# Threshold attention and a gated feed-forward block: every stage as tasks of one engine, ordered by a list scheduler

## The chip, the core and the metric

The kernel runs on one core of a Trainium2 chip. A core has a matrix engine (PE, with its weight loads listed as PEld), a vector engine (DVE), an engine for activation functions (ACT), a general engine (POOL) and SP, which here only issues DMAs. Each engine works through its own queue in the order in which the program was written, and waits at an instruction until the semaphores that it needs have arrived. The metric is the time of one execution in microseconds (us).

## What is computed

```python
# q, k, v: (8, 8, 576, 64) f32; 64 heads, two heads are one "pair"
scores = q @ k.T / sqrt(64)
thresh = max(scores, -1) - tau                 # tau = 0.02
scores = where(scores >= thresh, scores, -1e9)
attn   = exp(scores - max); attn /= sum(attn, -1) + 1e-9
x      = (attn @ v) reshaped to (4608, 512)
h      = x @ w_in                              # (512, 2048), given as 64-bit floats
g      = h * sigmoid(1.702 * h)
out    = g @ w_out                             # (2048, 512), given as 64-bit floats
```

## The kernel before

**Attention.** There are 32 pairs n (four for each of the eight sequences). Of the 576 keys, 512 are four main tiles t of 128 and the last 64 of both heads share one tail tile. For a pair, DVE transposes q and k (`prep`, L206); PE makes the scores with keys on the partitions (`scores`, L233 and L222) into PSUM tiles `ps` of the pool psA, which has three buffers; ACT copies them to SBUF (L239, L226) as `s_m` (seven buffers) or `s_t`. DVE takes the maximum over groups of 32 keys of each tile (`in_groups`, L254), folds the parts into one threshold a query (`over_groups`, `thresholds`) and spreads it over the partitions as `mb` (L282). Then DVE subtracts `mb` from each tile (`sub`, L291 and L294), and ACT runs a very steep Prelu, which is the mask, and the exp (`exps`, L300 and L301). When all five tiles are done, PE multiplies by the values (`values`, `pv`, L315). The row sums come, for the first six pairs (`BY_PE`), from a second pass of PE over the five tiles with a matrix of ones (`sums_by_pe`, `den`, also L315), which DVE then reads (L337), and for the others from DVE (`in_groups` again, as a sum). `place_x` (L366) multiplies `pv` by the reciprocal sums into `xT`.

**Feed-forward.** The 4608 rows are nine blocks of 512. A block needs the pairs of its sequences. It has 16 products with w_in (`mm1`, tile `hps`, L379), each of four matmuls in two parts; behind each, ACT makes a tanh (`th`, L386) and DVE the gated product `gT` (L387). Then it has four products with w_out (`mm2`, tile `ops`, L395) of 16 matmuls in eight parts, which ACT halves (`osb`, L401) and SP stores. `hps` and `ops` share the pool psM, which has two buffers. A matmul in f32 shows as two records in the trace: 128 records of hps and 128 of ops for each block.

**Weights.** w_in and w_out arrive as 64-bit floats and are converted in 64 pieces (`convert`): two DMAs, two DVE steps (L162, L172), one of ACT (L167), two of POOL (L176, L179), one of DVE (L188) and one of POOL (L192), with the piece that was begun one call earlier finished first.

**What sets the order.** All engines are scheduled by hand: what the program writes first stands first in each queue. A list `plan` holds (place, function) entries and is sorted by place. A pair begins at `LEN * n` with `LEN = 18`, and its steps stand at fixed distances from there, for instance

```python
at(t0 + 1.5 * t, scores, n, t)
at(t0 + 9.0 + 1.3 * t, exps, n, t)
at(t0 + 18.6, values, n)
```

The parts of a block are spread evenly between the moment at which its pairs are ready and that of the next block. A function of the plan writes for several engines at once: `exps` is Prelu and exp in a row, the second part of `mm1` also writes the tanh and gT, and `scores` also writes the copies.

Of the kernel before, what the change touches and what calls it, by code (L numbers as in the profile page):

```python
# [17 lines left out]
P = 128  # L18
GELU_SCALE = 1.702
EPS = 1e-9  # L20
# [8 lines left out]
def kernel(  # L29
# [66 lines left out]

    raws, vs = {}, {}

    def load_pair(n, queues):
        b, hp = divmod(n, NPAIR)  # L100
        raws[n] = []
        for (name, src), queue in zip((("q", q), ("k", k)), queues):
            t = work.tile([P, QB, 32], FP32, name=f"{name}_raw", tag=f"{name}_raw", bufs=1)
            for h in range(2):
                for j in range(2):
                    queue.dma_start(
                        out=t[ds(64 * h + 32 * j, 32), :, :],
                        in_=src[b, 2 * hp + h, :, ts(j, 32)].rearrange(
                            "(c p) d -> p c d", p=32
                        ),  # L110
                    )
            raws[n].append(t)
# [18 lines left out]
    staged, opened = [], []  # L131
    n_loaded = [0]

    def load_w():
        if n_loaded[0] == len(pieces):
            return
        dst, src, c, j = pieces[n_loaded[0]]
        n_loaded[0] += 1
        part = dst[:, c, ts(j, WC)]
        dram = src[ts(c, P), ts(j, WC)]  # L140
        if not wide:
            nc.sync.dma_start(out=part, in_=dram)
            return
# [9 lines left out]
        staged.append((t, t3, part))  # L153

    def convert_w():

        if not staged:
            return
        t, t3, part = staged.pop(0)
        hi = t[:, :, 1]  # L160
# [3 lines left out]
        )  # L164

        mant = work.tile([P, WC], FP32, name="mant", tag="mant")
        nc.scalar.activation(  # L167
            out=mant, in_=frac, func=AF.Copy, bias=1.0, scale=2.0**-28
        )

        ex = work.tile([P, WC], U32, name="ex", tag="ex")
        nc.vector.tensor_scalar(  # L172
            out=ex, in0=hi, scalar1=20, scalar2=0x7FF,
            op0=ALU.logical_shift_right, op1=ALU.bitwise_and,
        )
# [6 lines left out]
        opened.append((t, part, mant, ex))  # L182

    def convert_w_end():
        if not opened:
            return
        t, part, mant, ex = opened.pop(0)
# [4 lines left out]
        nc.gpsimd.tensor_tensor(out=part, in0=mant, in1=ex.bitcast(FP32), op=ALU.mult)  # L192

    def convert():
        convert_w_end()
        convert_w()
        load_w()


    mats, sT, stats, mbs = {}, {}, {}, {}  # L200

    def prep(n, which):

        src = raws[n][which]
        dst = work.tile([P, S], FP32, name="qkT", tag=f"qkT{which}", bufs=1)
        nc.vector.transpose(out=dst, in_=src.rearrange("p c d -> p (c d)"))  # L206
        mats.setdefault(n, []).append(dst)
        if which == 1:
            for h in range(2):
                nc.scalar.copy(out=kd[n % 2][ts(h, D), ts(h, D)], in_=dst[ts(h, D), MAIN:S])  # L210
            del raws[n]
# [4 lines left out]
    def scores(n, t):  # L216
        qT, kT = mats[n]
        if t == NKT:
            st = work.tile([P, S], FP32, name="s_t", tag="s_t", bufs=2)
            ps = psA.tile([P, 2, 512], FP32, name="ps", tag="ps")  # L220
            for c in range(2):
                nc.tensor.matmul(  # L222
                    ps[:, c, 0:SH], lhsT=kd[n % 2], rhs=qT[:, ts(c, SH)],
                    start=True, stop=True,
                )
            nc.scalar.copy(out=halves(st), in_=ps[:, :, 0:SH])  # L226
            del mats[n]
        else:
            st = work.tile([P, 2, S], FP32, name="s_m", tag="s_m", bufs=7)
# [8 lines left out]
            for h in range(2):  # L238
# [201 lines left out]

    LEN = 18.0
    BY_PE = 6
    plan = []
# [82 lines left out]
```

## Time and profile before

| | us |
|---|---|
| median of 3 runs (1716.7 to 1718.14) | 1717.1 |
| the profiled execution | 1718.59 |
| its span | 1716.8 |
| PE busy in the span | 1477.6 (86%) |
| DVE busy | 979.5 (57%) |
| ACT busy | 673.0 (39%) |
| POOL busy | 117.1 (7%) |

A busy time is the sum of an engine's instructions; for PE it contains the time in which matmuls run at a lower granted clock. The granted clock of a stretch is the share of TensorE's full speed. A wait is put down to the instruction whose semaphore came last.

### The profile page before, as it was taken

The page shows a single profiled execution, that of the slowest core. Times are in us where ns is not written, and L with a number is a line of the kernel's source. Part 1 is how long each engine was busy: PE and PEld are TensorE (multiplying, and loading weights), DVE is VectorE, ACT ScalarE, POOL GpSimd, SP SyncE. Part 2 cuts the span into 40 slices and gives each one's busy share as a digit, 9 for nine tenths or more (in the row PEclk, how much of TensorE's full clock was granted, in tenths as well). Part 3 has the DMA queues.
Part 4 walks back from the last instruction along what each step waited for, and adds up shares of the span by engine and source line. Part 5 has one row for each costly group of instructions (what it writes and reads, how often), then busy time and mean ns, then how long its engine had stood idle before and what let it go on. Part 6 is the DMA issues. An engine that isn't in the chain of part 4 may idle for free.

```text
span 1716.8 us, 14214 instructions
## 1 busy us (share of the span) xinstructions
PE 1477.6 (86%) x4976; PEld 677.1 (39%) x4976; DVE 979.5 (57%) x1698; ACT 673.0 (39%) x917; POOL 117.1 (7%) x204
## 2 busy tenths in 40 slices
PE   4647475799889978997899799998899789999998
PEld 2323132344334433443344344444344334444443
DVE  4664646486666666666577566766577567510110
ACT  4453424244344444444444433543444444310110
POOL 0014645400000000000000000000000000000000
PEclk8877787899989998999899999999899989999999
DMA  3215555411111111111111100210111110000000
GB/s 55 58 45 135 163 172 160 156 34 33 21 21 33 34 21 21 28 39 21 21 28 33 28 6 16 45 25 18 21 33 34 21 21 20 13 0 13 13 6 19
DMA packets 214295, 72.22 MB, mean 42 GB/s; under 512 B 193232, under 2 KB 201424, under 8 KB 214224
## 3 DMA queue, kind: packets, MB, share of 16 engines
q1 hardware_dynamic: 211856, 71.02, 16.8%
q8 instruction: 39, 0.64, 0.2%
q10 hardware_dynamic: 2368, 0.30, 0.1%
q14 instruction: 32, 0.26, 0.1%
HBM read 61.84 MB, written 9.44 MB: 42 GB/s over the span
## 4 chain that ended last, share of the span: by engine, by line
PE 66%; DVE 16%; ACT 9%; POOL 4%; issue 3%; DMA 1%; SPq 1%; DVEq 0%; POOLq 0%; ACTq 0%
PE ops L395 28%; PE hps L379 19%; PE pv L315 8%; PE ps L233 7%; DVE s_m L291 4%; ACT s_m L301 3%; ACT s_m L300 3%; DVE part L254 2%; PE den L315 2%; DVE gT L387 2%; ACT th L386 1%; PE ps L222 1%; DVE mb L282 1%; DVE qkT L206 1%; POOL ex L176 1%
## 5 line engine op out<-in xcount | busy, mean ns | idle before, releaser
L379 PE MATMUL hps<-xT,w_in 128*128 128x512 f32 x1152 | 580.1, 656 | 140.9 <-DVE gT L387 130.5
L395 PE MATMUL ops<-w_out,gT 128*128 128x512 f32 x1152 | 514.0, 597 | 2.1 <-ACT osb L401 2.1
L379 PEld LDWEIGHTS hps<-xT,w_in 128*128 128x128 f32 x1152 | 233.2, 209 | 452.8 <-issue 287.5
L254 DVE TRANSPOSE_TENSOR_REDUCE part<-s_m 128x36 f32<-128x1152 f32 x232 | 316.0, 1363 | 140.8 <-ACT s_m L239 132.3
L395 PEld LDWEIGHTS ops<-w_out,gT 128*128 128x128 f32 x1152 | 214.0, 190 | 269.3 <-issue 260.9
L387 DVE SCALAR_TENSOR_TENSOR gT<-th,hps 128x512 f32<-128x512 f32 x144 | 98.4, 684 | 371.7 <-ACT th L386 371.7
L239 ACT COPY s_m<-ps 128x576 f32<-128x576 f32 x256 | 150.8, 641 | 307.1 <-PE ps L233 307.1
L233 PE MATMUL ps<-qkT 64*128 64x288 f32 x1024 | 171.8, 442 | 65.7 <-DVE qkT L206 61.8
L300 ACT ACTIVATE s_m<-s_m 128x1152 f32<-128x1152 f32 x128 | 148.1, 1157 | 180.4 <-DVE s_m L291 180.0
L301 ACT ACTIVATE s_m<-s_m,shift,scl 128x1152 f32<-128x1152 f32 x128 | 172.4, 1347 | 4.3
L291 DVE TENSOR_TENSOR s_m<-s_m,mb 128x1152 f32<-128x1152 f32 x128 | 170.9, 1364 | 0.6
L233 PEld LDWEIGHTS ps<-qkT 64*128 64x128 f32 x1024 | 95.3, 192 | 175.3 <-issue 78.9
L386 ACT ACTIVATE th<-hps 128x512 f32<-128x512 f32 x144 | 85.0, 590 | 176.6 <-PE hps L379 176.6
L315 PE MATMUL pv<-s_m,v_m 128*64 128x288 f32 x1024 | 136.1, 420 | 0.1
L315 PEld LDWEIGHTS pv<-s_m,v_m 128*64 128x64 f32 x1024 | 72.4, 141 | 61.7 <-issue 15.4
L167 ACT ACTIVATE mant<-frac 128x256 f32<-128x256 uint32 x64 | 26.5, 414 | 128.5 <-DVE frac L162 128.5
L401 ACT ACTIVATE osb<-ops 128x512 f32<-128x512 f32 x36 | 21.2, 589 | 128.5 <-PE ops L395 128.5
L315 PE MATMUL den<-s_m,ones 128*64 128x288 f32 x192 | 32.8, 510 | 25.6 <-ACT s_m L239 25.6
L254 DVE TRANSPOSE_TENSOR_REDUCE part_t<-s_t 128x18 f32<-128x576 f32 x58 | 44.8, 772 | 14.0 <-ACT s_t L226 12.6
L188 DVE SCALAR_TENSOR_TENSOR ex<-w,ex 128x256 uint32<-128x256 uint32 x64 | 26.7, 418 | 43.7 <-POOL ex L179 43.4
L294 DVE TENSOR_TENSOR s_t<-s_t,mb 64x576 f32<-64x576 f32 x64 | 48.8, 763 | 0.4
L282 DVE STREAM_TRANSPOSE mb<-thr 128x1152 f32<-128x1152 f32 x32 | 44.1, 1378 | 1.1
(47 smaller groups left out, 619.9 us busy)
## 6 DMA issues: line engine op xcount, KB each, us to landing
q_raw<-in_q_dram SPq DMA_DIRECT2D x128, 72.0 KB, 2.5
out_dram<-osb SPq DMA_DIRECT2D x36, 256.0 KB, 2.1
k_raw<-in_k_dram SPq DMA_DIRECT2D x124, 72.0 KB, 2.5
v_m<-in_v_dram SPq DMA_DIRECT2D x64, 128.0 KB, 2.5
w<-in_moe_w_in_dram SPq DMA_DIRECT2D x32, 256.0 KB, 3.2
w<-in_moe_w_out_dram SPq DMA_DIRECT2D x32, 256.0 KB, 2.9
w64s<-in_moe_w_in_dram SPq DMA_DIRECT2D x32, 255.6 KB, 3.5
w64s<-in_moe_w_out_dram SPq DMA_DIRECT2D x32, 255.6 KB, 3.3
```

The source lines that it names most:

```text
L233: nc.tensor.matmul(ps[h][:, c, 0:SH], lhsT=kT[ts(h, D), ts(t, P)], rhs=qT[ts(h, D), ts(c, SH)], start=True, stop=True,)
L239: nc.scalar.copy(out=halves(st[:, h, :]), in_=ps[h][:, :, 0:SH])
L254: nc.vector.tensor_reduce(out=o, in_=i, axis=AXL.X, op=op, apply_transpose=True)
L282: nc.vector.transpose(out=mb.rearrange("p h s -> p (h s)"), in_=f.unsqueeze(2).to_broadcast([P, 2 * QB, 32]),)
L291: nc.vector.tensor_tensor(out=s, in0=s, in1=mb, op=ALU.subtract)
L300: nc.scalar.activation(out=s, in_=s, func=AF.Prelu, alpha=STEEP)
L301: nc.scalar.activation(out=s, in_=s, func=AF.Exp, scale=scl, bias=shift)
L315: nc.tensor.matmul(o[ts(h, D), c, 0:SH], lhsT=lhsT, rhs=rhs, start=(t == 0), stop=(t == NKT),)
L379: nc.tensor.matmul(hidden[0], lhsT=w_in[:, c, ts(j, P)], rhs=xTs[blk][:, c, :], start=(c == 0), stop=(c == NDC - 1),)
L386: nc.scalar.activation(out=th, in_=hidden[0], func=AF.Tanh, scale=GELU_SCALE / 2)
L387: nc.vector.scalar_tensor_tensor(out=gT[j], in0=th, scalar=1.0, in1=hidden[0], op0=ALU.add, op1=ALU.mult)
L395: nc.tensor.matmul(acc[0], lhsT=gT[j][:, ts(i, P)], rhs=w_out[:, j, :], start=(j == 0), stop=(j == NFC - 1),)
```

## The change

The plan of places is gone. Each step is now a task of one engine with an estimated cost, a rank, the tasks that it comes after, and what it takes from and gives back to counted pools (`psA`, `psM`, `s_m` and so on; the pools keep their sizes, only the small tiles `part_t` and `red` have three buffers). `run_in_order` plays the tasks through in the builder: each engine, when free, starts the ready task with the lowest rank whose pools have room, and the order of these starts is the order in which the program is written. Nothing of this runs on the chip. Steps that were one function are split: the copies (`keep`), the mask and the exp, the tanh, gT (`gelu`), the halving, the store, the fold of the maxima, and the five steps of a conversion.

Ranks: tanh, gT, halving and store come first (-1), a pair's steps have the rank of the pair, the pieces of weights lie between 3.2 and 4.2, and the products of the feed-forward part come last (1000), so PE takes them whenever no attention is ready. The scores of pair n also wait for the part 16 x (n - 6) of the feed-forward list.

For the first four pairs, `den` and `pv` are made tile by tile, each behind its own exp, with `den` in two tiles of psM; pairs 4 to 7 have `den` as before, in psA, so that eight pairs instead of six have their sums from PE. The reduce of `den` is two instructions of half the size.

```diff
+    def task(engine, cost, rank, f, *a, after=(), take=(), give=(), lag=0.06):
+        tasks.append((engine, cost, rank, f, a, [x for x in after if x is not None],
+                      take, give, lag))
...
+            for engine, queue in ready.items():
+                if engine in busy:
+                    continue
+                for rank, i in sorted(queue):
+                    take = tasks[i][6]
+                    if all(free[pool] >= take.count(pool) for pool in set(take)):
+                        break
+                else:
+                    continue
...
+                busy.add(engine)
+                heapq.heappush(events, (now + tasks[i][1], 0, i))
+                tasks[i][3](*tasks[i][4])
...
+    def sums_by_pe(n, tiles, apart):
+        if 0 not in tiles:
+            ps = pss[n]
+        elif apart:
+            ps = [psM.tile([P, BLK], FP32, name="den", tag="mo") for _ in range(2)]
...
+        by_values(n, lambda t, h: ones, lambda h: ones_t[:, h, :], ps, tiles)
...
+        a = task("SP", 1.1, rank, load_w, i, take=("w64",), lag=3.5)
+        a = task("DVE", 0.6, rank, cv_open, i, after=[a], take=("cv",))
+        m = task("ACT", 0.42, rank, cv_mant, i, after=[a])
+        e = task("POOL", 0.82, rank, cv_exp, i, after=[a])
+        a = task("DVE", 0.42, rank, cv_sign, i, after=[e], give=("w64",))
+        ready_w.append(task("POOL", 0.75, rank, cv_end, i, after=[a, m], give=("cv",)))
...
+                ffn.append(task(
+                    "PE", 1.8, LAST, mm1, blk, j, p, after=after,
+                    take=("psM",) if p == 0 else (), give=("xT",) if last else (),
+                ))
+            a = task("ACT", 0.6, FIRST, tanh, j, after=ffn[-1:], take=("io",))
+            gelus[j] = task(
+                "DVE", 0.7, FIRST, gelu, j, after=[a, last_mm2.get(j // 2)],
+                give=("psM", "io"),
+            )
...
-        t0 = LEN * n
+        gate = per_pair * (n - LEAD)
+        after = ffn[gate : gate + 1] if gate >= 0 else []
...
-            at(t0 + 1.5 * t, scores, n, t)
-            at(t0 + 1.5 * t + 1.0, in_groups, n, t, ALU.max)
-            at(t0 + 8.7 + 1.3 * t, sub, n, t)
-            at(t0 + 9.0 + 1.3 * t, exps, n, t)
...
+            a = task("ACT", 0.7 if tail else 1.17, r, mask, n, t, after=[a])
+            ws.append(task("ACT", 0.88 if tail else 1.36, r, exps, n, t, after=[a]))
...
+        if n < NPAIR:
+            pv = den = None
+            for t in every:
+                first = t == 0
+                den = task(
+                    "PE", 1.1, r, sums_by_pe, n, [t], True, after=[ws[t], den],
+                    take=("psM", "psM") if first else (),
+                )
+                pv = task(
+                    "PE", 1.1, r, values, n, [t], after=[ws[t], den, pv, lv],
+                    take=("psA",) if first else (), give=(back[t],) if t < NKT else ("s_t", "v_m"),
+                )
```

Three places show what the order now is. The first is ACT while a block's products with w_in run beside attention (`th` is the tanh, the other rows are mask and exp of a pair's tiles). Before, in the sixth block:

```order
L386 ACTIVATE th<-hps 128x512 x2
L300 ACTIVATE s_m<-s_m 128x1152
L301 ACTIVATE s_m<-s_m,shift,scl 128x1152
L300 ACTIVATE s_m<-s_m 128x1152
L301 ACTIVATE s_m<-s_m,shift,scl 128x1152
L386 ACTIVATE th<-hps 128x512
L300 ACTIVATE s_m<-s_m 128x1152
L301 ACTIVATE s_m<-s_m,shift,scl 128x1152
```

After, in the fifth block:

```order
L475 ACTIVATE th<-hps 128x512
L370 ACTIVATE s_m<-s_m 128x1152
L475 ACTIVATE th<-hps 128x512
L374 ACTIVATE s_m<-s_m,shift,scl 128x1152
L370 ACTIVATE s_m<-s_m 128x1152
L475 ACTIVATE th<-hps 128x512
L374 ACTIVATE s_m<-s_m,shift,scl 128x1152
L370 ACTIVATE s_m<-s_m 128x1152 x2
L475 ACTIVATE th<-hps 128x512
```

The tanh of the next product has moved ahead of the exp of a tile, and later ahead of the exps of two. The second place is DVE beside the same rows (`gT` is the gated product, `s_m<-s_m,mb` a sub, `part<-s_m` a reduce). Before:

```order
L282 STREAM_TRANSPOSE mb<-thr 128x1152
L387 SCALAR_TENSOR_TENSOR gT_73<-th,hps 128x512
L291 TENSOR_TENSOR s_m<-s_m,mb 128x1152 x2
L387 SCALAR_TENSOR_TENSOR gT_74<-th,hps 128x512
L291 TENSOR_TENSOR s_m<-s_m,mb 128x1152
L206 STREAM_TRANSPOSE qkT<-q_raw 128x576
L254 TENSOR_REDUCE part<-s_m 128x36
L291 TENSOR_TENSOR s_m<-s_m,mb 128x1152
L206 STREAM_TRANSPOSE qkT<-k_raw 128x576
L387 SCALAR_TENSOR_TENSOR gT_75<-th,hps 128x512
```

After:

```order
L478 SCALAR_TENSOR_TENSOR gT_74<-th,hps 128x512
L361 TENSOR_TENSOR s_m<-s_m,mb 128x1152 x3
L478 SCALAR_TENSOR_TENSOR gT_75<-th,hps 128x512
L361 TENSOR_TENSOR s_m<-s_m,mb 128x1152
L318 TENSOR_REDUCE part<-s_m 128x36
L478 SCALAR_TENSOR_TENSOR gT_76<-th,hps 128x512
L364 TENSOR_TENSOR s_t<-s_t,mb 64x576 x2
L318 TENSOR_REDUCE part<-s_m 128x36
L478 SCALAR_TENSOR_TENSOR gT_77<-th,hps 128x512
L318 TENSOR_REDUCE part<-s_m 128x36 x2
L478 SCALAR_TENSOR_TENSOR gT_78<-th,hps 128x512
```

Between two gT stand at most three large steps, and the transposes of the next pair's q and k have moved out of this stretch. The third place is DVE behind the first pair's threshold. Before:

```order
L282 STREAM_TRANSPOSE mb<-thr 128x1152
L291 TENSOR_TENSOR s_m<-s_m,mb 128x1152 x3
L206 STREAM_TRANSPOSE qkT<-q_raw 128x576
L291 TENSOR_TENSOR s_m<-s_m,mb 128x1152
L206 STREAM_TRANSPOSE qkT<-k_raw 128x576
L294 TENSOR_TENSOR s_t<-s_t,mb 64x576 x2
L337 TENSOR_REDUCE r<-den 128x18
```

After (`ex`, `frac` and `w_...` belong to the conversion of weights):

```order
L352 STREAM_TRANSPOSE mb<-thr 128x1152
L318 TENSOR_REDUCE part<-s_m 128x36
L361 TENSOR_TENSOR s_m<-s_m,mb 128x1152
L318 TENSOR_REDUCE part<-s_m 128x36
L361 TENSOR_TENSOR s_m<-s_m,mb 128x1152
L241 SCALAR_TENSOR_TENSOR ex<-w_177,ex 128x256
L361 TENSOR_TENSOR s_m<-s_m,mb 128x1152
L241 SCALAR_TENSOR_TENSOR ex<-w_183,ex 128x256
L361 TENSOR_TENSOR s_m<-s_m,mb 128x1152
L213 TENSOR_SCALAR frac<-w64s 128x256
L217 TENSOR_SCALAR ex<-w_195 128x256
```

Reduces of the second pair and steps of the conversion now stand between the subs of the first, ahead of the reduce of `den` (in after L417, some rows further on).

## Rows read from the trace of the kernel before

**Rows 1.** Chain that ended last, by time: start us, us, what, count.
```profile
38.02 4.88 PE den L315 x40
...
440.67 6.66 PE hps L379 x8
...
1396.77 6.47 PE hps L379 x8
...
1489.70 54.93 PE hps L379 x128
...
1657.36 54.95 PE ops L395 x128
```

**Rows 2.** PE timeline, two pairs: start, us, what, count [idle before <-releaser].
```profile
1080.28 1.24 PE L233 MATMUL ps<-qkT 64*128 64x288 f32 x8
...
1119.19 1.24 PE L233 MATMUL ps<-qkT 64*128 64x288 f32 x8
...
1154.78 3.70 PE L379 MATMUL hps<-xT,w_in 128*128 128x512 f32 x8 [3.48 <-DVE gT L387]
1164.21 6.70 PE L379 MATMUL hps<-xT,w_in 128*128 128x512 f32 x8 [5.73 <-DVE gT L387]
1170.84 1.24 PE L233 MATMUL ps<-qkT 64*128 64x288 f32 x8
```

**Rows 3.** Timelines of ACT (two rows) and DVE inside the slower pair.
```profile
1148.54 1.17 ACT L300 ACTIVATE s_m<-s_m 128x1152 f32<-128x1152 f32 x1 [3.43 <-DVE s_m L291]
...
1153.43 0.58 ACT L386 ACTIVATE th<-hps 128x512 f32<-128x512 f32 x1
...
1154.04 0.69 DVE L387 SCALAR_TENSOR_TENSOR gT<-th,hps 128x512 f32<-128x512 f32 x1 [4.26 <-ACT th L386]
```

**Rows 4.** PE timeline, the first product of the feed-forward part.
```profile
157.36 1.98 PE L379 MATMUL hps<-xT,w_in 128*128 128x512 f32 x4
```

**Rows 5.** Windows: busy of PE, PEld, DVE, ACT, POOL; granted clock; DMA.
```profile
55.26:88.24 32.98, 20.17 (x116) 11.14 (x116) 19.81 (x31) 16.88 (x21) 0.00 (x0) 0.76 0.30 75
...
157.00:356.00 199.00, 139.23 (x440) 61.58 (x438) 117.96 (x275) 73.88 (x128) 99.66 (x169) 0.85 0.49 152
```

**Rows 6.** DVE groups by form: count, busy us, mean ns, idle before.
```profile
L254 DVE TRANSPOSE_TENSOR_REDUCE part<-s_m 128x36 f32<-128x1152 f32 x232 | 316.0, 1363 | 140.8 <-ACT s_m L239 132.3 <-ACT s_m L301 7.2
...
L291 DVE TENSOR_TENSOR s_m<-s_m,mb 128x1152 f32<-128x1152 f32 x128 | 170.9, 1364 | 0.6
...
L188 DVE SCALAR_TENSOR_TENSOR ex<-w,ex 128x256 uint32<-128x256 uint32 x64 | 26.7, 418 | 43.7 <-POOL ex L179 43.4
...
L172 DVE TENSOR_SCALAR ex<-w 128x256 uint32<-128x256 uint32 x64 | 18.8, 294 | 0.0
L162 DVE TENSOR_SCALAR frac<-w64s 128x256 uint32<-128x256 uint32 x64 | 18.3, 285 | 13.7 <-DMA w64s<-in_moe_w_in_dram 9.1 <-DMA w64s<-in_moe_w_out_dram 4.5
```

**Rows 7.** DVE timeline, the first two pairs.
```profile
22.01 1.38 DVE L282 STREAM_TRANSPOSE mb<-thr 128x1152 f32<-128x1152 f32 x1
...
42.92 0.78 DVE L337 TRANSPOSE_TENSOR_REDUCE r<-den 128x18 f32<-128x576 f32 x1 [11.58 <-PE den L315]
...
53.88 1.38 DVE L282 STREAM_TRANSPOSE mb<-thr 128x1152 f32<-128x1152 f32 x1
```

**Rows 8.** Waits: line <- releaser: us in total, times, longest us.
```profile
DVE ex L188 <- POOL ex L179: 43.4, 38, 1.6
```

**Rows 9.** Timelines of POOL (two rows) and DVE while weights are converted.
```profile
117.04 0.40 POOL L176 TENSOR_SCALAR ex<-ex 128x256 uint32<-128x256 uint32 x1 [115.13 <-DVE ex L172]
...
126.91 1.39 POOL L176 TENSOR_SCALAR ex<-ex 128x256 uint32<-128x256 uint32 x1
...
126.16 1.88 DVE L291 TENSOR_TENSOR s_m<-s_m,mb 128x1152 f32<-128x1152 f32 x1
```

**Rows 10.** PE timeline and window near the end, after attention.
```profile
1575.46 14.00 PE L395 MATMUL ops<-w_out,gT 128*128 128x512 f32 x32 [0.69 <-ACT osb L401]
...
1550.00:1600.00 50.00, 47.94 (x111) 20.65 (x110) 0.00 (x0) 1.79 (x3) 0.00 (x0) 1.00 0.04 16
```

More of the change, by code (lines that the diff above doesn't have):

```diff
@@ L1 @@
+import heapq
 import math
@@ L97, with load_qk @@
     raws, vs = {}, {}
-    def load_pair(n, queues):
+    def load_qk(n, which, queue):
         b, hp = divmod(n, NPAIR)
[L101 to L112, printed above, removed]
+        name, src = (("q", q), ("k", k))[which]
+        t = work.tile([P, QB, 32], FP32, name=f"{name}_raw", tag=f"{name}_raw", bufs=1)
+        for h in range(2):
+            for j in range(2):
+                queue.dma_start(
+                    out=t[ds(64 * h + 32 * j, 32), :, :],
+                    in_=src[b, 2 * hp + h, :, ts(j, 32)].rearrange("(c p) d -> p c d", p=32),
+                )
+        raws[n, which] = t
@@ L392, in mm2, with gelu @@
+    def gelu(j):
+        nc.vector.scalar_tensor_tensor(
+            out=gT[j], in0=ths.pop(j), scalar=1.0, in1=hidden.pop(j), op0=ALU.add, op1=ALU.mult
+        )
+    def mm2(i, part):
         if part == 0:
-            acc[0] = psM.tile([P, d_model], FP32, name="ops", tag="mo")
+            acc[i] = psM.tile([P, d_model], FP32, name="ops", tag="mo")
         for j in range(2 * part, 2 * part + 2):
             nc.tensor.matmul(
-                acc[0], lhsT=gT[j][:, ts(i, P)], rhs=w_out[:, j, :],
+                acc[i], lhsT=gT[j][:, ts(i, P)], rhs=w_out[:, j, :],
@@ new lines @@
+    FIRST, LAST = -1.0, 1000.0
+    BY_PE = 8
+    LEAD = 6
+    ready_w = []
+    for i in range(len(pieces)):
+        rank = NPAIR - 0.8 + i / len(pieces)
+        if not wide:
+            ready_w.append(task("SP", 0.6, rank, load_w, i, lag=2.5))
+            continue
+        a = task("SP", 1.1, rank, load_w, i, take=("w64",), lag=3.5)
[4 more added lines that the diff above has]
+        ready_w.append(task("POOL", 0.75, rank, cv_end, i, after=[a, m], give=("cv",)))
@@ new lines, with feed_forward @@
+    tau_done = task("DVE", 1.0, -2.0, tau_terms)
+    placed, ffn = {}, []
+    last_mm2 = {}
+    def feed_forward(blk):
+        b = -(-(blk + 1) * BLK // S) - 1
+        xs = [placed[n] for n in range(NPAIR * (b + 1))]
+        for j in range(NFC):
+            for p in range(2):
+                after = ffn[-1:] + xs[-NPAIR:]
+                if blk == 0:
+                    after += [ready_w[(j * P // WC) * NDC + c] for c in (2 * p, 2 * p + 1)]
+                last = j == NFC - 1 and p == 1
+                ffn.append(task(
[6 more added lines that the diff above has]
+                give=("psM", "io"),
+            )
+        for i in range(BLK // P):
+            for p in range(NFC // 2):
+                after = ffn[-1:] + [gelus[2 * p], gelus[2 * p + 1]]
+                if blk == 0:
+                    n_in = d_ff // WC * NDC
+                    per = d_model // WC
+                    after += ready_w[n_in + per * 2 * p : n_in + per * (2 * p + 2)]
+                ffn.append(task(
+                    "PE", 1.8, LAST, mm2, i, p, after=after, take=("psM",) if p == 0 else (),
+                ))
+                last_mm2[p] = ffn[-1]
+            a = task("ACT", 0.6, FIRST, half, i, after=ffn[-1:], take=("io",), give=("psM",))
+            task("SP", 0.6, FIRST, store, blk, i, after=[a], give=("io",), lag=2.2)
@@ L502 @@
+    run_in_order()
 _INS = ['q', 'k', 'v', 'tau', 'moe_w_in', 'moe_w_out']
```

413 lines of the change are left out of this document (240 added, 173 removed).

## The prediction

> **What bounds the kernel now.** I read the windows by stage first, then PE's timeline over two neighbouring pairs, then ACT and DVE inside the slower of the two, then the first 160 us. Prices come from the profiled execution: 1718.6 us, of which 1716.8 are span; the runs' median of 1717.1 lies 1.5 below it.
>
> PE is the bound, but it does not work all the time. Its work at full clock: the last block runs undisturbed, 128 hps records in 54.93 and 128 ops records in 54.95 [rows 1], so a block costs 109.9 and nine cost 989. A pair that lies beside ops takes 38.91 (scores at 1080.28 to scores at 1119.19) [rows 2] without a wait; 64 of its records are ops, 27.5, so a pair's attention costs PE 11.4, switching included, and 32 pairs 366. Six pairs have sums on PE at 4.88 each [rows 1], 29. Together 1384 of the 1717: 333 us are lost.
>
> Where? The pair beside hps takes 51.65 (1119.19 to 1170.84), 12.7 more, with two waits of 3.48 and 5.73 for gT, and eight records that take 6.70 instead of 3.70 at a lower clock [rows 2]. The chain of waits has twelve of these slow groups of eight, from 440.67 to 1396.77 [rows 1], one for each such pair, so some 150 us. The cause is an order [rows 3]: a tanh of 0.58 is issued at 1153.43 after two pairs of mask and exp, the first of which waited 3.43 for DVE before it ran from 1148.54; gT waits for that tanh, and PE for gT, since psM has two buffers. The other 180 are lost in the first 356 us: hps starts at 157.36 [rows 4], and from there to 356 PE is busy for 139 of 199 at a granted clock of 0.85 [rows 5].
>
> **Part 1, the order in the steady stages.** Nothing is computed differently there. The order of after has one mask or exp, at most two, between two tanh on ACT, and 3.4 to 4.7 us of DVE work between two gT: three subs and a gT are 3 x 1.34 + 0.69 = 4.7, a sub, a reduce and a gT 1.34 + 1.36 + 0.69 = 3.4, two reduces and a gT the same [rows 3, 6] (a sub is its group's 170.9 through 128). Over the four steps gT_74 to gT_78 shown in the section on the change that is about 14.9 against 4 x 3.43 = 13.7 of PE. The 1.2 is within what two psM buffers give (one hps, 3.43), and outside such a burst PE has attention as well and DVE catches up. The bounds of what remains of the 150 are 0 and 150; I take 15, a few tenths per gT in the 112 gT of the seven blocks that have attention beside them. The wait that may come instead is the same one, gT, with half a microsecond where it had four. Queued behind a late gT on DVE are the reduces and subs of the next pair; these have slack, since pairs may run up to six ahead of the blocks.
>
> **Part 2, the first four pairs.** Before, DVE stands still for 11.58 in each of these pairs, waiting for den, because all 40 records of values and then 40 of den (4.88) come after the last exp [rows 1, 7]. From one threshold (mb) to the next is 31.87 (22.01 to 53.88), and DVE works 19.81 of the next one [rows 5, 7]. After, den and values follow tile by tile behind each exp, so two of these ten steps remain behind the last, and the next pair's scores and reduces are put between the subs (third place in the section on the change). The row sums then go through two psM tiles, free at that time. The reduce of den is cut in two, a few tenths more. DVE becomes the bound of this stage: 19.8 per pair plus what of the conversion is put there. A conversion costs DVE 0.285 + 0.294 + 0.418 = 1.0 [rows 6].
> Walk: the first mb ended at 22.01 + 1.38 = 23.4; now two openings, two transposes and a reduce stand ahead of it, partly in former waits: 26. Then three times 19.8 plus 3, 5 and 5.5 conversions plus waits of 2.5 to 3 (for ACT, whose mask and exp follow each sub, and for den): 52, 79, 107. The rest of pair 3 is 10.3, with 5.5 conversions, two transposes and 2 of waiting: its placement ends near 127. Before, the first hps started at 157.4. Bounds: 110 if DVE never waited, 150 if all the old waits stayed and only the last were covered.
>
> **Part 3, the conversion of the weights.** At that point 20 of 64 pieces are converted by the order, in waits that DVE had anyway. From there to the last piece DVE has 44 x 1.0 = 44, sixteen gT at 0.69 = 11, and 47 of attention (pairs 4 and 5 at 19.8 and the start of pair 6): 102. PE has for the same stretch about 100 of work (block 0's hps, and ops that each need their four pieces), so neither can wait for the other for free; I go by DVE. To it I add 15: DVE waited 43.4 for POOL in 38 of 64 conversions, 0.7 per piece [rows 8], 30 for 44 pieces, of which I let half be covered since two pieces are now in flight with other work between; zero and 70 (1.6, the longest wait, on each) are the bounds. So the last piece is there at 127 + 102 + 15 = 244, with POOL's last product 245. The loads change their order on SP but not their number; they wait for the same three buffers.
> DVE and POOL disturb each other: a sub of 1.88 (126.16) instead of 1.34, and beside it a POOL step of 1.39 instead of 0.40 [rows 6, 9]. This grows, as 28 subs now lie beside conversions; half of the 0.54 for each is 8 and is in the 15, all of it would be 15. [...]
>
> **The sum.** At 245, by the order, PE has done block 0's hps (54.9), 28 ops records (12.0), six whole pairs with den (6 x 16.3 = 97.9) and the scores of a seventh (half of 11.4): 170.5. Its whole work is 1384 plus two more den (pairs 6 and 7, 9.8) = 1394. Left: 1223.5, bound by PE. 245 + 1223.5 + 15 = 1483.5; behind PE's end come 4.5 (1712.3 to 1716.8) [rows 1]; 1.8 around the span; less 1.5 to the median: **1488 us**. Taking sums off DVE for pairs 6 and 7 frees DVE in a stage where it is not the bound and counts as nothing there; its cover is PE's work, and without that it would be a gain.
>
> **Rivals.**
> 1. The conversion is the new wait: DVE's queue is fixed and a step "open, sign" without work between stands still for POOL. [...] For it: 38 waits of this kind in before [rows 8]. Against: two pieces in flight. Chance 0.14.
> 2. Half of the steady waits stay, because mean durations order the queues and each in-order queue passes its delay to the others: 75 instead of 15, 1548. For it: DVE has only a few tenths of slack per gT in a burst. Chance 0.10.
> 3. Slower than before. [...] Chance 0.03.
> 4. The order in the program is not what the chip does in the start: pairs remain a chain of some 32 each. Then pair 3 is placed at 150, the conversions fill the waits instead, and the time is about 1500: inside the range of the forecast.
>
> **How the numbers follow.** Forecast, with rival 4 in it: 0.71, from 1460 (no waits beyond the work) to 1525. Rivals 1 and 2 lie at 1525 to 1590; they are 0.24 together, and up to 1560 about half of that is taken in. Rival 3 has 0.03; no change within 0.2%, about what a measurement of this kernel can tell from none, 0.01; below 1460 0.01. The range is 1460 to 1560; faster 0.96, same 0.01, slower 0.03.
>
> **What would show it.** Right: the first hps near 127 us, the last product of w_out on POOL near 245, PE busy for nearly all of the time from there on with a granted clock of 1.00, waits of hps for gT under 25 us in total, no wait of DVE for den above 3, and pairs beside hps as short as those beside ops, about 39. Wrong: waits of DVE for POOL above 40 in total (rival 1), waits of hps of 2 us and more in every block (rival 2), a granted clock under 0.95 in the steady blocks (rival 3), mb to mb of 32 at the start (rival 4).

## The result, and the profile after

The changed kernel takes **1497.2 us** (median of 4 runs, 1496.2 to 1500.0) where the kernel before takes 1717.0; the ratio is 0.872, with a 95% interval of 0.871 to 0.874. Predicted were 1488, range 1460 to 1560. The profiled execution took 1496.9, of which 1495.0 are span.

The page of the changed kernel, its busy times and the granted clock in 40 slices, then the two large groups (busy, mean ns | idle before, releaser) and, from the page of the kernel before, its group of hps (L379):

```profile
PE 1423.8 (95%) x5056; PEld 662.6 (44%) x5056; DVE 973.9 (65%) x1678; ACT 653.8 (44%) x917; POOL 124.5 (8%) x204
...
PE   5758897999999999999999999999999999999998
...
PEclk8888998999999999999999999999999999999999
...
L486 PE MATMUL ops<-w_out,gT 128*128 128x512 f32 x1152 | 516.7, 600 | 10.8 <-POOL w_out L249 9.9
L467 PE MATMUL hps<-xT,w_in 128*128 128x512 f32 x1152 | 514.5, 598 | 4.0 <-DVE gT L478 2.5
...
L379 PE MATMUL hps<-xT,w_in 128*128 128x512 f32 x1152 | 580.1, 656 | 140.9 <-DVE gT L387 130.5
```

The hole is at the start only. The group of hps now reads like that of ops: 598 ns a record and 4.0 us of idle time, while before it had 656 ns and 140.9. Three windows of the changed kernel (length; busy time of PE, PEld, DVE, ACT, POOL; granted clock; DMA share; GB/s) separate the stages:

```profile
0.00:133.70 133.70, 86.15 (x488) 47.44 (x488) 104.96 (x196) 76.83 (x111) 43.95 (x71) 0.85 0.51 122
133.70:264.20 130.50, 110.70 (x403) 50.47 (x402) 103.51 (x220) 61.77 (x108) 80.50 (x134) 0.95 0.65 190
...
300.00:1275.00 975.00, 974.89 (x3514) 452.74 (x3514) 727.68 (x1207) 475.51 (x639) 0.00 (x0) 1.00 0.14 29
```

From 300 to 1275 PE is busy for 974.89 of 975 us at a granted clock of 1.00; [rows 5] showed 0.85 for 157 to 356. PE's timeline of the changed kernel has the points that the prediction named: the first hps, the two longest waits for a piece of w_out, and a run of hps in a later block (start, us, what, count):

```profile
135.48 1.98 PE L467 MATMUL hps<-xT,w_in 128*128 128x512 f32 x4
...
231.37 2.08 PE L486 MATMUL ops<-w_out,gT 128*128 128x512 f32 x2 [5.68 <-POOL w_out L249]
...
264.25 2.08 PE L486 MATMUL ops<-w_out,gT 128*128 128x512 f32 x2 [3.10 <-POOL w_out L249]
...
1034.69 20.76 PE L467 MATMUL hps<-xT,w_in 128*128 128x512 f32 x48
```

In the last row 48 records run without a stop. In [rows 2] the same stretch of a pair had stops of 3.48 and 5.73 and eight records in 6.70 instead of 3.70.

The start on DVE, thresholds (`mb`) of the first four pairs and the placement of the fourth:

```profile
26.98 1.34 DVE L352 STREAM_TRANSPOSE mb<-thr 128x1152 f32<-128x1152 f32 x1
...
53.46 1.33 DVE L352 STREAM_TRANSPOSE mb<-thr 128x1152 f32<-128x1152 f32 x1
...
82.22 1.34 DVE L352 STREAM_TRANSPOSE mb<-thr 128x1152 f32<-128x1152 f32 x1
...
110.54 1.37 DVE L352 STREAM_TRANSPOSE mb<-thr 128x1152 f32<-128x1152 f32 x1
...
132.86 0.88 DVE L455 TENSOR_TENSOR xT<-pv,rc 128x288 f32<-128x288 f32 x3
```

From mb to mb it is 26.5, 28.8 and 28.3, after 31.9 in [rows 7]. What DVE waited for between the placement of pair 3 and the last piece of weights (133.7 to 264.2; us in total, times, longest), and POOL's last product:

```profile
DVE ex L241 <- POOL ex L235: 15.4, 22, 1.6
DVE frac L213 <- DMA w64s<-in_moe_w_out_dram: 8.2, 7, 1.9
...
DVE frac L213 <- DMA w64s<-in_moe_w_in_dram: 0.9, 2, 0.7
```

```profile
263.47 0.72 POOL L249 TENSOR_TENSOR w_out<-mant,ex 128x256 f32<-128x256 f32 x1 [0.43 <-DVE ex L241]
```

So the last piece is there at 264.2, and from then on PE waits for nothing.

### The profile page after: what moved, and what is told of

Its sections match the earlier page's. It is cut to its first block, busy times and chain, and to the rows that moved or that the text cites. A ratio compares the mean times of both kernels' runs of the same rounds, so it can differ in the third digit from the quotient of the medians.

```text
span 1495.0 us, 14337 instructions
## 1 busy us (share of the span) xinstructions
PE 1423.8 (95%) x5056; PEld 662.6 (44%) x5056; DVE 973.9 (65%) x1678; ACT 653.8 (44%) x917; POOL 124.5 (8%) x204
## 3 DMA queue, kind: packets, MB, share of 16 engines
q1 hardware_dynamic: 211856, 71.02, 19.6%
## 4 chain that ended last, share of the span: by engine, by line
PE 85%; DVE 6%; POOL 2%; ACT 2%; DMA 2%; issue 2%; SPq 1%; POOLq 0%; DVEq 0%; ACTq 0%
PE ops L486 33%; PE hps L467 30%; PE pv L388 10%; PE ps L285 9%; PE ps L276 2%; PE den L388 1%; POOL ex L232 1%; DMA w64s<-in_moe_w_out_dram 1%; DVE ex L241 1%; ACT s_m L374 1%; ACT s_m L370 1%; POOL ex L235 1%; DMA w64s<-in_moe_w_in_dram 1%; DVE part L318 1%; DVE qkT L259 1%
## 5 line engine op out<-in xcount | busy, mean ns | idle before, releaser
L467 PE MATMUL hps<-xT,w_in 128*128 128x512 f32 x1152 | 514.5, 598 | 4.0 <-DVE gT L478 2.5
L318 DVE TRANSPOSE_TENSOR_REDUCE part<-s_m 128x36 f32<-128x1152 f32 x224 | 304.1, 1367 | 152.7 <-ACT s_m L304 144.2
L467 PEld LDWEIGHTS hps<-xT,w_in 128*128 128x128 f32 x1152 | 213.5, 190 | 269.8 <-issue 244.3
L374 ACT ACTIVATE s_m<-s_m,shift,scl 128x1152 f32<-128x1152 f32 x128 | 168.9, 1340 | 0.6
L370 ACT ACTIVATE s_m<-s_m 128x1152 f32<-128x1152 f32 x128 | 145.2, 1156 | 45.3 <-DVE s_m L361 44.8
L285 PEld LDWEIGHTS ps<-qkT 64*128 64x128 f32 x1024 | 98.7, 200 | 134.6 <-issue 52.9
L388 PE MATMUL den<-s_m,ones 128*64 128x288 f32 x256 | 37.2, 430 | 23.5 <-ACT s_m L374 21.7
L241 DVE SCALAR_TENSOR_TENSOR ex<-w,ex 128x256 uint32<-128x256 uint32 x64 | 31.8, 498 | 21.5 <-POOL ex L235 21.3
L232 POOL TENSOR_SCALAR ex<-ex 128x256 uint32<-128x256 uint32 x64 | 39.5, 617 | 70.0 <-DVE ex L217 68.0
```

Source lines behind the costliest of these rows:

```text
L232: nc.gpsimd.tensor_scalar(out=ex, in0=ex, scalar1=1150.0, scalar2=896.0, op0=ALU.min, op1=ALU.max)
L285: nc.tensor.matmul(ps[h][:, c, 0:SH], lhsT=kT[ts(h, D), ts(t, P)], rhs=qT[ts(h, D), ts(c, SH)], start=True, stop=True,)
L318: nc.vector.tensor_reduce(out=o, in_=i, axis=AXL.X, op=op, apply_transpose=True)
L370: nc.scalar.activation(out=s, in_=s, func=AF.Prelu, alpha=STEEP)
L374: nc.scalar.activation(out=s, in_=s, func=AF.Exp, scale=scl, bias=shift)
L388: nc.tensor.matmul(o[c][ts(h, D), 0:SH], lhsT=lhsT, rhs=rhs, start=(t == 0), stop=(t == NKT),)
```

## The experiments

### Part 2 undone in the changed kernel, and done alone in the kernel before

First the changed kernel with the tile-by-tile sums and values of the first four pairs taken out:

```diff
-        if n < NPAIR:
+        if n < 0:
...
-        if NPAIR <= n < BY_PE:
+        if n < BY_PE:
```

> The changed kernel with one part undone: the first four pairs have den and values whole, behind the last exp, den in psA, as pairs 4 to 7 have them. Theory (part 2 of the prediction): each of these pairs becomes a chain again, 31.9 from mb to mb instead of the 26.5 to 28.8 measured in the changed kernel, so the first hps comes about 21 later, near 157 instead of 135.5; the waits that come back are partly filled with conversions, so the last piece (264 now) moves by less, 5 to 15, and the time is 1507 to 1522 instead of 1497. Rival (the list order alone fills the waits, the tiles bring nothing): first hps within 5 of 135 and 1494 to 1500.

Measured: 1516.8 us, ratio to the kernel before 0.883 (0.882 to 0.885). That is 19.6 more than the changed kernel takes, in the range that was expected for the loss of this part. DVE of that kernel:

```profile
26.80 1.34 DVE L352 STREAM_TRANSPOSE mb<-thr 128x1152 f32<-128x1152 f32 x1
...
66.01 1.37 DVE L352 STREAM_TRANSPOSE mb<-thr 128x1152 f32<-128x1152 f32 x1
```

The details were not as expected. A pair takes 39.2, not 31.9, and the list puts conversions into its waits: 26 pieces are done by 133.7, against 19 in the changed kernel. The first hps comes at 178.3, 43 later. The last piece, however, is there at 253, earlier than 264. From there PE waits for nothing in this kernel too, but it has 1257 us left, against 1227 at 264.2. The lesson is that neither event alone is the bound of the start: what counts is how much of its work PE has done by the time from which it never waits again.

The same part alone in the kernel before, at the places of its plan:

```diff
+            if n < NPAIR:
+                at(t0 + 9.1 + 1.3 * t, den_tile, n, t)
+                at(t0 + 9.1 + 1.3 * t, values, n, [t])
```

> The kernel before with part 2 alone: in the first four pairs the plan puts den (in two tiles of psM) and values of a tile behind its exp; everything else, the places of the conversions too, stays. Theory: the wait of DVE for den (11.58 in each of these pairs) shrinks to 3 to 5, mb to mb from 31.9 to about 25, the first hps from 157 to about 130; what follows is the same stage of conversion and the same steady stage, so the time is 1717 - 27 = 1690 (1680 to 1700). Rival (the conversion's fixed places are the bound of the start, and what the pairs save is waited for there): 1712 to 1718.

Measured: 1704.5 us, ratio 0.992 (0.991 to 0.994); 13 faster, half of what was expected. The first hps comes at 146.2, not near 130. Its DVE:

```profile
22.01 1.38 DVE L282 STREAM_TRANSPOSE mb<-thr 128x1152 f32<-128x1152 f32 x1
38.00 0.94 DVE L339 TRANSPOSE_TENSOR_REDUCE r<-den 128x9 f32<-128x288 f32 x2 [6.66 <-PE den L315]
...
46.85 1.38 DVE L254 TRANSPOSE_TENSOR_REDUCE part<-s_m 128x36 f32<-128x1152 f32 x1 [1.62 <-ACT s_m L239]
...
52.81 1.38 DVE L282 STREAM_TRANSPOSE mb<-thr 128x1152 f32<-128x1152 f32 x1
```

The wait for den shrinks by 4.9, from 11.58 [rows 7] to 6.66, but the pair only from 31.9 to 30.8. Of the 4.9, 3.45 come back as three waits of the next pair's reduces for ACT's copies of the scores (the 1.62 above, 1.53 and 0.30). And 6.66 are left, since the plan has nothing for DVE between the last sub and the reduce of den. In this kernel, cutting den into tiles is worth 13 without an order that also puts the next pair's scores and reduces there.

### What in the order made the steady stages slow

The prediction's cause was a tanh that stands behind two pairs of mask and exp on ACT. The first try gave tanh and gT the worst rank but the products' own:

```diff
-            a = task("ACT", 0.6, FIRST, tanh, j, after=ffn[-1:], take=("io",))
+            a = task("ACT", 0.6, 500.0, tanh, j, after=ffn[-1:], take=("io",))
...
-                "DVE", 0.7, FIRST, gelu, j, after=[a, last_mm2.get(j // 2)],
+                "DVE", 0.7, 500.0, gelu, j, after=[a, last_mm2.get(j // 2)],
```

> The changed kernel with one number changed in two places: tanh and gT have a rank behind every step of attention (500) instead of ahead of them (-1). Nothing is computed differently. Theory (the waits of hps in the kernel before came from tanh and gT standing behind attention): waits of hps for gT come back, 4.0 of idle time before hps becomes 60 to 140, with a lower granted clock in the steady blocks, and the time is 1560 to 1650. Rival (the steady stages became dense because attention and blocks are interleaved in smaller steps by the list, whatever the rank of the tanh): 1495 to 1505 and idle time before hps under 10.

Measured: 1562.0 us, ratio 0.909 (0.908 to 0.911). The time is in the expected range, but for another reason, and the granted clock of the steady blocks did not fall. Windows of this kernel for the conversion and for the steady stages:

```profile
133.70:356.00 222.30, 157.16 (x653) 75.46 (x654) 154.71 (x299) 101.06 (x158) 86.07 (x134) 0.84 0.43 123
500.00:1300.00 800.00, 791.24 (x2796) 362.42 (x2795) 591.92 (x975) 381.77 (x513) 0.00 (x0) 1.00 0.13 27
```

```profile
PE hps L467 <- DVE gT L478: 51.8, 3, 23.2
...
PE hps L467 <- DVE gT L478: 4.8, 10, 0.5
```

The waits (the first row is 133 to 356, the second from 500 on) lie in the conversion stage, where DVE has attention or a piece to do for 43.5 of these 51.8 us and gT comes last: three waits, one of 23.2. In the steady stages, where DVE has idle time, the rank costs 9 of 800 us. So the rank of tanh and gT does not explain the 150 us.

Next, coarser tasks: mask and exp of two tiles as one task, so that up to 5.06 of ACT's work stand ahead of a tanh, as in the kernel before, but none queued before its sub is done by the builder's estimate.

```diff
+            if t % 2 == 0 and not tail:
+                continue
+            us = range(t - 1, t + 1) if not tail else [t]
+            a = task("ACT", 1.58 if tail else 5.06, r, both, n, us, after=[a])
+            ws += [a] * len(us)
```

> The changed kernel with coarser tasks on ACT: mask and exp of two tiles are one task of 5.06 that is written when both subs are done, so up to four of these instructions stand ahead of a tanh, but none of them is queued before its sub is done. Nothing is computed differently. Theory A (how many masks and exps stand ahead of a tanh decides, as the prediction has it): the waits of hps for gT return in each of the seven blocks beside attention, 40 to 100 in total, and the time is 1560 to 1640. Theory B (what decides is a mask at the head of ACT's queue whose sub is not done; seen in e2, where after 500 us only 4.8 of such waits were left although tanh ranked last): hps waits after 500 us stay under 15, the start loses 10 to 30 since exps come later there, and the time is 1505 to 1535.

Measured: 1523.2 us, ratio 0.887 (0.885 to 0.888): theory B's range. After 500 us:

```profile
PE hps L472 <- DVE gT L483: 15.1, 15, 2.4
```

15 waits of 1.0 on average are at most the price of the number of masks and exps, a tenth of the 150. At most, because the estimates are not exact: a mask still waits for its sub at the head of the queue 8 times after 500 us, 13.3 in all.

The direct test is one number in the kernel before. Mask and exp move two places later; their spacing stays, and so does their number between two tanh:

```diff
-            at(t0 + 9.0 + 1.3 * t, exps, n, t)
+            at(t0 + 11.0 + 1.3 * t, exps, n, t)
```

> The kernel before with one number changed: mask and exp of the five tiles stand 2.0 places later in the plan (11.0 instead of 9.0), the spacing of 1.3 stays, and so does the number of masks and exps between two tanh. DVE's order does not change. Theory B (a mask that waits at the head of ACT's queue for its sub holds up the tanh behind it): ACT's wait of masks for subs (114 after 500 us) falls below 40, most of the waits of hps for gT (83.6 after 500 us) go, and the time is 1570 to 1640. Theory A (two pairs of mask and exp between two tanh, 5.06 of work, are too much by themselves): waits of hps stay above 60 and the time is 1690 to 1720.

Measured: **1604.8 us**, ratio 0.934 (0.932 to 0.936), so 113 us less from this one number. ACT's wait of masks for subs after 500 us, 126 before, is gone; that of hps for gT is 27.1 (10 times) instead of 83.6 (20 times). Theory B holds: what delayed the tanh was mainly a mask that had reached the head of ACT's queue before its sub was done, as in the first row of [rows 3] with its 3.43, and not the work of two masks and exps. The trace bears the comparison out. From the first hps of the second block to that of the eighth (406.7 to 1489.5 before, 399.1 to 1372.9 here) 109 of the 113 are gained, and in both stretches 24 of the 96 tanh have two masks and two exps ahead of them, 12 have one of each. ACT of this kernel shows where the 27.1 come from:

```profile
1068.85 1.17 ACT L300 ACTIVATE s_m<-s_m 128x1152 f32<-128x1152 f32 x1
1070.05 1.35 ACT L301 ACTIVATE s_m<-s_m,shift,scl 128x1152 f32<-128x1152 f32 x1
1071.30 1.15 ACT L300 ACTIVATE s_m<-s_m 128x1152 f32<-128x1152 f32 x1
1072.48 1.35 ACT L301 ACTIVATE s_m<-s_m,shift,scl 128x1152 f32<-128x1152 f32 x1
1075.86 0.50 ACT L210 COPY kd<-qkT 64x64 f32<-64x64 f32 x2 [2.03 <-DVE qkT L206]
1076.38 0.60 ACT L386 ACTIVATE th<-hps 128x512 f32<-128x512 f32 x1
```

It is the same thing with another instruction: the copy `kd` waits 2.03 at the head of the queue for DVE's transpose, and the tanh behind it is late. Each of the ten stops has such a copy ahead of it, with a wait of 2.03 or 2.04. The tanh's own input was there: PE's run of hps (36 records from 1059.43) had ended at 1075.04, before the copy began at 1075.86, and still the tanh ran behind the copy, at 1076.38.

A weaker form of the same idea had been tried before that, in the kernel before: sub, mask and exp, and sum 1.9 places apart instead of 1.3.

```diff
-            at(t0 + 8.7 + 1.3 * t, sub, n, t)
-            at(t0 + 9.0 + 1.3 * t, exps, n, t)
+            at(t0 + 8.7 + 1.9 * t, sub, n, t)
+            at(t0 + 9.0 + 1.9 * t, exps, n, t)
```

> The kernel before with part 1 done in another way: in the plan the sub, mask and exp, and sum of the five tiles of a pair stand 1.9 places apart instead of 1.3 (the fold of the sums moves from 18.7 to 20.1). A tanh comes every two places, so mostly one pair of mask and exp stands between two tanh instead of mostly two. Theory (the waits of hps are the order on ACT): most of the 150 that the twelve pairs beside hps lose goes, 1717 - 110 = 1607 (1580 to 1640), and the idle time before hps falls from 140.9 to under 50. Rival (gT is late because DVE reaches it late, behind subs, reduces and sums, and the places of mask and exp don't matter): 1700 to 1720, idle time before hps above 120.

Measured: 1659.7 us, ratio 0.966 (0.965 to 0.968); 58 faster, half of what was expected and in neither theory's range, and idle time before hps 99.8. ACT and PE of this kernel:

```profile
1106.62 1.17 ACT L300 ACTIVATE s_m<-s_m 128x1152 f32<-128x1152 f32 x1 [3.43 <-DVE s_m L291]
...
1109.07 0.58 ACT L386 ACTIVATE th<-hps 128x512 f32<-128x512 f32 x1
...
1114.28 0.50 ACT L210 COPY kd<-qkT 64x64 f32<-64x64 f32 x2 [2.20 <-DVE qkT L206]
```

```profile
1110.42 3.70 PE L379 MATMUL hps<-xT,w_in 128*128 128x512 f32 x8 [1.05 <-DVE gT L387]
1118.59 6.36 PE L379 MATMUL hps<-xT,w_in 128*128 128x512 f32 x8 [4.46 <-DVE gT L387]
```

Only one mask and exp stand ahead of the first tanh, and yet the mask waits the same 3.43 for its sub. That this run gave half is what led to the test above.

Both small edits together, those of e4 and e9, in the kernel before:

```diff
-            at(t0 + 9.0 + 1.3 * t, exps, n, t)
+            at(t0 + 11.0 + 1.3 * t, exps, n, t)
+            if n < NPAIR:
+                at(t0 + 11.1 + 1.3 * t, den_tile, n, t)
+                at(t0 + 11.1 + 1.3 * t, values, n, [t])
```

> The kernel before with two small edits in its plan: mask and exp 2.0 places later (e9) and den and values tile by tile in the first four pairs (e4). Theory: they act in different stages and add up, 1717 - 113 - 13 = 1591 (1583 to 1598); what is left to the changed kernel is then the stage of the conversions and the last waits of hps. Rival (the later exps of the first pairs take back what the tiles gave there): 1600 to 1607.

Measured: 1590.7 us, ratio 0.927 (0.926 to 0.929). They add up. Two local edits of the old plan bring 126 of the 220 us; the remaining 93 between this kernel and the changed one (idle time before hps is still 63.8, and the last piece comes at 325) were not divided further.

### How much slack the new order has

Each tanh of the changed kernel twice, in the same order:

```diff
+        for _ in range(2):
             nc.scalar.activation(out=ths[j], in_=hidden[j], func=AF.Tanh, scale=GELU_SCALE / 2)
```

> The changed kernel with each tanh issued twice (same values into the same tile); the order of all engines stays. It prices a gT that is 0.6 late each of 144 times. Theory (psM's two buffers give PE one hps, 3.43, of lead, of which tanh and gT need some 1.3, and ACT is idle for over half of the steady stages): PE's waits after 500 us stay under 15 and the time is 1497 to 1515. Rival (the steady stages have no slack per gT beyond some tenths): 0.6 for each gT beside attention, 112 of them, so 1550 to 1570.

Measured: 1505.3 us, ratio 0.877 (0.875 to 0.878): 8 more for 144 x 0.6 = 86 more of ACT. PE's waits for gT after 264 us are 5.6 (9 times, longest 0.9), the granted clock from 500 to 1300 stays 1.00. The two buffers of psM cover most of a gT that is 0.6 late.

Two den passes less, so that pairs 6 and 7 have their sums from DVE again:

```diff
-    BY_PE = 8
+    BY_PE = 6
```

> The changed kernel with BY_PE = 6: pairs 6 and 7 have their sums from DVE, as in the kernel before. Theory (from 264 us on PE is dense, so each us of its work is a us of the time): two passes of den less, 2 x 4.88 = 9.8, and 1487. Rival (DVE needs the relief in 264 to 404, where it is busy for 79 of 104, and its sums of five tiles each hold up the pairs): 1493 to 1500.

Measured: 1488.1 us, ratio 0.867 (0.865 to 0.868): 9.1 less, against 9.8 expected. From 264 us on the time is PE's work and nothing else, and this part of the change cost what it added.

### What bounds the start

POOL's first step of a conversion, the clamp of the exponent, left out:

```diff
-        nc.gpsimd.tensor_scalar(
-            out=ex, in0=ex, scalar1=1150.0, scalar2=896.0, op0=ALU.min, op1=ALU.max
-        )
```

> The changed kernel without POOL's first step of a conversion (the clamp of the exponent, 64 steps, 0.62 each on average); the order of all engines stays. Theory (the 130 us from the first hps to the last piece are bound by DVE with its waits for POOL, and its lengthened steps beside POOL): DVE's waits for POOL fall from 21.3 to under 9, the last piece comes at 248 to 256 instead of 264, and the time is 1485 to 1491 instead of 1497. Rival (the loads are the bound; DVE waits for them 9.1 in that stage already): the waits go over to the loads, the last piece stays after 260, the time 1494 to 1499.

Measured: 1489.3 us, ratio 0.868 (0.867 to 0.870). DVE's waits up to 300 us:

```profile
DVE frac L213 <- DMA w64s<-in_moe_w_out_dram: 13.7, 12, 1.7
...
DVE ex L238 <- POOL ex L232: 8.8, 18, 1.0
```

The waits for POOL fall from 21.3 to 8.8, those for the loads of w_out rise from 8.2 to 13.7, and the last piece comes at 256.5 instead of 264.2: 7.7 earlier, and the time is 7.9 less. The theory holds, and the rival has a share: part of what POOL gives back goes to the loads.

A version that uses this: three pieces of the conversion in flight instead of two, without more memory, fewer den passes, and the estimates of the builder set to the trace.

```diff
-               "raw0": 1, "raw1": 1, "qkT0": 1, "qkT1": 1, "v_m": 2, "w64": 3, "cv": 2}
+               "raw0": 1, "raw1": 1, "qkT0": 1, "qkT1": 1, "v_m": 2, "w64": 3, "cv": 3}
...
-        mant = work.tile([P, WC], FP32, name="mant", tag="mant")
+        mant = cv[i][1].bitcast(FP32)
...
-    BY_PE = 8
-    LEAD = 6
+    BY_PE = 6
+    LEAD = 8
...
-        rank = NPAIR - 0.8 + i / len(pieces)
+        rank = NPAIR - 1.2 + 1 * i / len(pieces)
...
-        e = task("POOL", 0.82, rank, cv_exp, i, after=[a])
+        e = task("POOL", 1.05, rank, cv_exp, i, after=[a])
```

> The changed kernel with the start relieved: three pieces of the conversion in flight instead of two (the mantissa is written into the tile of the fraction, so no memory is added), BY_PE = 6, LEAD = 8, the weights' rank 0.4 lower, and the costs of the conversion's tasks and of the feed-forward parts set to what the trace shows (POOL 1.05 and 0.9 instead of 0.82 and 0.75, DVE 0.66 and 0.55 instead of 0.6 and 0.42, PE 1.72 instead of 1.8). Theory (the last piece bounds the start, and DVE's 15.4 of waits for POOL are too short a lookahead): these waits fall below 8, the last piece comes at 245 to 255 instead of 264, and with the 9.8 of den the time is 1473 to 1484. Rival (POOL, busy for 80 of the 130 us of that stage, and the loads are the bound there): the last piece stays at 260 or later and only the den is gained, 1487.

Measured: **1477.8 us**, ratio to the kernel before 0.861 (0.859 to 0.862), 19 less than the changed kernel and 10 less than with BY_PE = 6 alone. DVE of this kernel waits 13.3 for POOL, more than the 8 expected, and the last piece comes at 254.4, within what was expected:

```profile
253.68 0.72 POOL L249 TENSOR_TENSOR w_out<-frac,ex 128x256 f32<-128x256 f32 x1 [0.83 <-DVE ex L241]
```

Which of its numbers brings the 10 was not taken apart.

## Why the prediction was right, and where it was not

The forecast's direction and mechanism held, the cause of the steady waits only in part. Its 1488 was 9 short, and that it was so close is partly luck: 19 too little in the start and 15 too much in the steady stages nearly cancelled. The terms:

| term | predicted | measured |
|---|---|---|
| pair 3 placed | 127 | 133.7 |
| from there to the last piece | 118 | 130.5 |
| PE's work left then | 1223.5 | 1227.1 |
| waits of the steady stages | 15 | 0 |
| behind PE's end | 4.5 | 3.7 |
| around the span, and to the median | +0.3 | +2.2 |

PE's last record ends at 1491.3, so 1227.1 and 3.7 lie before and behind it. The differences are +6.7, +12.5, +3.6, -15, -0.8 and +1.9, together 9.

**Part 1.** The 150 us went completely, where 15 were left in; hps waits 4.0 in all, under the 25 that were named as the sign. The cause was half right. The order of ACT was the cause, but the prediction read [rows 3] as too much work ahead of the tanh and argued with the number of masks and exps between two tanh. That number costs at most about 15 (e3); what cost most was the 3.43 in the same row, an instruction at the head of an in-order queue whose input is not there (e9). Nor did the order after have "at most two" of them between two tanh: the last gap shown in the section on the change has three. The list scheduler acts on the real cause as it is built: it starts a task, and so writes it, only when the tasks that it comes after are done by its estimate, and does something else on that engine until then. Since these are estimates, the masks' wait for subs does not go to nothing. ACT's masks, before and after:

```profile
L300 ACT ACTIVATE s_m<-s_m 128x1152 f32<-128x1152 f32 x128 | 148.1, 1157 | 180.4 <-DVE s_m L291 180.0
...
L370 ACT ACTIVATE s_m<-s_m 128x1152 f32<-128x1152 f32 x128 | 145.2, 1156 | 45.3 <-DVE s_m L361 44.8
```

Of the 44.8 that are left, 37.3 lie after 264.3. They hold up no tanh for which PE stops, since PE does not wait there. That 0 were left and not 15 fits e8: the prediction feared bursts of a few tenths per gT, and 0.6 on every gT costs 8.

**Part 2.** Right in kind: it is worth 19.6 (e1). DVE's wait for den in the first four pairs is gone, and rival 4 is refuted by its own sign: 26.5, 28.8 and 28.3 from mb to mb, not 32 (its time of 1500 came about for other reasons). The term was mis-sized by 6.7: the first mb ended 2.3 later than walked (28.3 instead of 26), the three steps from mb to mb took 0.5, 1.8 and 0.3 more, and the rest of pair 3 another 1.8. From the first mb to the placement DVE waits 6.9 for copies of the scores and 5.8 for POOL. And it is not separate from part 1: without an order that fills the gap, the tiles gave 13 (e4).

**Part 3.** DVE's work between the placement and the last piece was 103.5 (102 predicted), its waits for POOL 15.4 (15 predicted). Some luck is in both. The steps of the 44 conversions took 50.0 instead of 44, which leaves about 43 for attention instead of 47, and the 15 had been meant to hold the lengthened subs too. The step that failed is the sentence on the loads: they were costed at nothing because their number does not change. DVE waited 9.1 for them there, and e6 shows that they are the next bound behind POOL. Rival 1 did not come: 21.3 of waits for POOL over the whole start, not above 40.

**Subs beside POOL.** The prediction counted half of 0.54 for each of 28 subs. Of the 24 subs of main tiles in the first 264 us, five lost the whole of it (1.88 to 1.89); the others took 1.32 to 1.54. Two pairs of rows, each a sub of DVE and the POOL step that it meets; in the first pair POOL began first, in the second DVE:

```profile
217.02 1.88 DVE L361 TENSOR_TENSOR s_m<-s_m,mb 128x1152 f32<-128x1152 f32 x1
...
112.20 1.35 DVE L361 TENSOR_TENSOR s_m<-s_m,mb 128x1152 f32<-128x1152 f32 x1
```

```profile
216.84 0.84 POOL L249 TENSOR_TENSOR w_out<-mant,ex 128x256 f32<-128x256 f32 x1 [1.37 <-DVE ex L241]
217.77 1.39 POOL L232 TENSOR_SCALAR ex<-ex 128x256 uint32<-128x256 uint32 x1
...
112.38 1.44 POOL L232 TENSOR_SCALAR ex<-ex 128x256 uint32<-128x256 uint32 x1 [0.89 <-DVE ex L217]
```

The sub at 217.02 begins while POOL's product runs and is 0.54 longer; POOL's next step of 0.40 then ends 0.26 after the sub. The sub at 112.20 begins 0.18 ahead of POOL's step and keeps its 1.35; the step takes 1.44 instead of 0.40 and ends 0.27 after the sub. All five of the long subs begin behind a product of POOL like the first, and ten of the others ahead of a step of POOL like the second; in the two pairs the one that begins second loses more time, 0.54 of the sub against 0.12 of the product (0.84 instead of 0.72), and 1.04 of the step against nothing of the sub. Seven subs meet no step of POOL, and two (1.54 and 1.35) are mixed. The prediction's 15, for all of the 0.54 on each sub, let DVE be the loser in all 28; in ten of 24 POOL was, whose loss reaches DVE only through its waits for POOL. The loss on DVE that grew was that of the conversion's own steps, from 63.8 (26.7 + 18.8 + 18.3 in [rows 6]) to 74.4.

**The sums of pairs 6 and 7.** Counted as 9.8 of PE's work and no gain: 9.1 measured (e7).

**Rival 3** did not come: from 300 to 1275 the granted clock is 1.00. A late gT in the kernel before cost 6 on average: the four stops of a block last 3.48, 5.73, 3.48 and 4.04, and the eight records behind them take 0, 3.0, 1.7 and 2.8 longer than 3.70. What stops of this length do to the clock is taken up below.

## What to carry to other kernels

Where a fixed order feeds in-order queues, look on the engine ahead of the late one for the instruction with an idle time in brackets, and not only for the amount of work: an instruction that is queued before its input is there delays everything behind it, and moving it later by one number was worth 113 of 1717 us here. Such an idle time costs only where something late stands behind it; the changed kernel has 37.3 us of it on ACT after 264.3, where PE is dense. When an order is remade, cost the resources whose number of uses stays the same as well (here the loads), since a faster consumer meets them sooner: in e6 DVE's waits for the loads of w_out rose from 8.2 to 13.7. Once the bound engine has no gap left, each us of work that was moved to it to relieve another engine is paid in full (in e7, 9.1 us for 9.8 of work) and should be taken back.

## What the runs showed of the hardware

What a stop of PE cost beyond itself in these runs does not follow from its length alone: behind one of 3.48 it was 0 or 1.7. The table has all stops before hps of the given length after 500 us, with the time of the eight records behind each and the granted clock of those records. Eight records at a granted clock of 1.00 take 3.70. The clocks between 0.5 and 1.0 of the kernel before are mixtures of two levels: in windows of 0.46 us the eight records at 1206.43 have 1.00, then 0.50 from 1208.27 to 1211.03, then 1.00 again, and those at 1164.21 have 0.50 up to 1170.19.

| stop, us | kernel | eight records behind, us | granted clock |
|---|---|---|---|
| 2.71 to 2.72 | e9 | 3.70 (seven times), 5.40 (three times) | 1.00 and 0.68 |
| 3.48 to 3.49 | before | 3.70 and 5.40, by turns | 1.00 and 0.68 |
| 4.03 to 4.04 | before | 6.47 | 0.57 |
| 4.46 | e5 | 5.08 to 6.45 | 0.57 to 0.72 |
| 5.73 | before | 6.69 to 6.70 | 0.55 |

Rows of e9, and of the kernel before:

```profile
751.16 5.40 PE L379 MATMUL hps<-xT,w_in 128*128 128x512 f32 x8 [2.72 <-DVE gT L387]
...
1077.75 3.70 PE L379 MATMUL hps<-xT,w_in 128*128 128x512 f32 x8 [2.71 <-DVE gT L387]
```

```profile
1206.43 5.40 PE L379 MATMUL hps<-xT,w_in 128*128 128x512 f32 x8 [3.48 <-DVE gT L387]
```

All stops of 4.0 and more in these rows brought the lower level (in the kernel before 0.55 to 0.57 over the eight records), those of 2.7 to 3.5 only some of the time (0.68 or 1.00). In the changed kernel's conversion stage the stop of 3.10 at 264.25 was followed by two records at 0.50. What decides in the middle range was not tested.

In e3, 15 stops of up to 2.4 between products leave the granted clock of 500 to 1300 at 1.00, with PE busy for 781 of 800. In the kernel before, with 16 stops of 3.48 to 5.73 in the same window, it is 0.96.
